# A fused attention and expert kernel: the written order of the first two batches replaced, v loaded behind k, no idle products

## The chip, the cores and the metric

The kernel runs on one core of one Trainium2 chip. A NeuronCore has five engines with instruction streams of their own: TensorE (PE, matrix products, with its weight loads shown as PEld), VectorE (DVE), ScalarE (ACT), GpSimd (POOL) and SyncE (SP, which here issues every DMA). The metric is the device time of one execution in microseconds, the median of several runs; smaller is better.

## The reference

Two attentions, then a layer with three gates, in float32:

```python
def sm_attn(qq, kk, vv):
    s = scale * np.matmul(qq, kk.transpose(0, 1, 3, 2))
    s = s - np.max(s, axis=-1, keepdims=True)
    a = np.exp(s)
    a = a / (np.sum(a, axis=-1, keepdims=True) + 1e-09)
    return np.matmul(a, vv)
p_packed = sm_attn(p, k, v)                 # 32 packed queries per head
out = sm_attn(q, p_packed, p_packed)        # 576 queries per head
x = out.transpose(0, 2, 1, 3).reshape(B * S, H * D)
h = np.maximum(np.maximum(x @ w1, x @ w2), x @ w3)
return h @ w_out
```

There are 8 batches of 8 heads, 576 positions and head dimension 64; w1 to w3 are 512 by 768 and w_out is 768 by 512.

## The kernel before, in words

All of the work of one batch is cut into stages. A stage is a Python generator that emits a few instructions at each step, and the order in which steps of different stages and batches are emitted is written out by hand as a text of words: START for all of batches 0 and 1 and the beginning of batch 2, and LOOP, which is run for each of the batches 2 to 7 with numbers relative to it. `run` (L619) reads the words. A word is a letter for the stage, digits for its batch (added to the loop's base) and its part, and perhaps a last letter for the engine of a step that has a choice: v for VectorE, g for GpSimd, a for ScalarE. Without that letter the step takes a default. Each engine runs its instructions in the order in which they were emitted, so this text sets every queue. The words stand for:

- k, v, q, w: loads on SP's queue. One k tile (L159) holds keys and packed queries of half the heads (640 KB), one q tile (L174) 576 KB, one v pair (L165, L166) 512 and 64 KB, one w tile (L153) 512 KB of raw weights, three for each of the six parts of w1 to w3 and six more for w_out. w tiles have six buffers in turn; k, v, q and several intermediate results share eight.
- C: a raw w tile is turned into float32 without a table: two ScalarE steps (L188, L193), a shift on VectorE (L202), an integer add on GpSimd (L206).
- S: scores of the packed queries (L253, tiles s1, two halves r = 0 and 1). A: maximum (L266, L267) and exponential (L271), then, for batches 0 and 1, transposes on TensorE (L296, L297) and copies (L129 on ACT, L131 on DVE). X: from batch 2 on the transposes go by VectorE (L313) and sixteen small DMAs (L319). Z: reciprocal (L282, L283). V: value products (L337) and their scaling (L347). K: transpose of the packed result (L352) and a copy to pt.
- Q: products of q with the packed result (L366). B: the second softmax, in blocks of 32 (L389 to L412), its result split into a rounded high and a low part (a2h, a2l).
- P: the packed result times part j of the weights (L439), split in ph and pl (L450, L452). N: the layer products mi (L475), three for each of the two halves r, because high times high, low times high and high times low are added up; 216 for a batch. E: the maximum over three gates (L489). H: sums and differences of quarters and their splits, O: the products with w_out (L544, mo) in the seven-product scheme of Strassen, F: their sums and the stores. W prepares w_out for that.
- I and J with a count of 128-column blocks: idle products. `rouse` (L138) multiplies the identity with itself into a PSUM tile that the next real product overwrites. I arms it ahead of the next stage's products, J emits it at once. START has I10, J9, J6, three times J2, J11 and J21.

PSUM has a pool of four tiles of one bank ("moe": mi, mo, and some pw) and one of two tiles of two banks ("big").

Of the kernel before, what the change touches and what calls it, by code (L numbers as in the profile page):

```python
# [45 lines left out]


START = """
k00 k01 I10 S0 A00 A00 J9 A00 q00 A00 w00 A01 A01 v00 J6 A01 v01 Z01 C00 C00 Z00 w02 C02 A01v V00 C00 V00 q01
V01 V01 J2 K0 C00 w01 w10 K0 C02 C02 J2 Q0 B010 C02 B010 B010v C01 C01 w11 B010 C10 C01 C01 Q0 w12 C10 B001  # L50
B000 B001 B000 B001v B000v C10 C10 C11 C11 C11 B000 C11 B000 B010 w20 C12 J11 P00 P00 w22 B011 P00 B000 B000
C12 B011 B001 P00 C12 C12 J21 P01 k10 B000 B000 B010 B001 C20 w32 k11 w21 B000 B000 B010 B001 N00 B010 B010
B010g C22 C22 P01 P00 B010 N00 B001 B011v B001g v11 J2 S1 v10 B011 P01 C32 C32 N01 N01 N01 C20 B011 w30 E000v
C22 B011v B001 E010 A11 A11 A10 A10 E010 Z11 B001v C21 C20 C21 C22 N00 B001v B011 E000 A10 A11 q10 A10v E000
q11 A11 N00 B011g B011 B011 V101 C20 C30 C30 w31 B011 Z10 E010 N01 V101 C21 C21 K1 C30 N00 w52 C31 K1v C32 C32
Q1 N00 E011 E001 B10 C31 w41 P02 P02 B11 C52 P10 P10 B10 w40 B11 k20 C40 C41 C31 P02 N01 E011 C30 N01 C31 P03
B10 P03 E001 E001 C41 N02 N02 E020 N02 C52 N02 E011 k21 N02 H00 w42 B10 B11 P10 E021 P03 S2 C40 E020 C40 N03
N03 N03 v21 C41 C41 C42 E020 B11 C42 B10 E021 C52 E030 C42 A20 A20 A21 A21 w50 C50 w51 B11 B11 B10 X2 X2 C50
C50 C51 N02 C52 N03 C40 C42 P04 C51 C50 B10 E030 E030 P11 B11 N03 B11g N03 C51 B10g P04 C51 P04 E031 N04 N04
N04 P05 E031 B11 v20 B11 E040v E040 B10 H01 H01v N04 N04 N04 E021 w61 C61 E031 P05 E041 P05 N05 N05 N05 E040  # L60
w60 C60 B10g B10 B11 H00 N10 C61 E041 P11 Z20 E050 H00v X2 C60 C60 E041 C61 E050 P11 V201 Z21 V201 N11 N11 K2
w64 N10 C61 E110v E110 E050 H01 H01 w65 C65 C65 N11 q21 N11 N10 K2 E100v N10 H04v H04 q20 Q2 N11 w62 N10 E111
E110 C60 W0v N10 W0v W0v W0 w63 W0 H02v H02 E101 C65 P13 H04v B20 E100 B21 E101 C65 W0 E111 E100 P12 N11 C62
C62 C63 C63 P13 C62 P12 W0v H03 C64 N05 C63 E101 N05 N05 C63 E051v P12 E051 C64 C64 P13 N12 N12 E111 C62 H01
H03v W1v W1v W1v N13 H02v N13 N13 E120 E130 P14 W1 P15 P15 E130 N12 C64 W2 W2 E051 N12 E121 W1v N13 E131 E130
P14 W2v W2g W0 P15 E120 E120 N13 E131 W2v N12 E121 N12 E121 W0g W0 H05g P14 W2g O0 O0 W1 W2v B21 W2 N14 N14
W1v B20 N13 E131 H03 H05 F0 E140 O0 E140 F0 N14 E140 H12v H03v O0 k31 F0 N14 H05 N14 N15 N15 N15 B20v H11 H05v
E141 N14 E141 H01v W2 H10v W1v E150 B21v E150 E141 H03 F0 H03v W1g N15 N15 E151 E151 O0 H10g H10v H05 O0 H05v
O0 B21 E150 W2 F0 F0 H13 H13 N15 E151 H14v O0 F0 F0 O0 B20 F0 O0 O0 B20 W1v H12 O0 F0 H12 H14 H11 F0 F0 F0 O0
H13v O0 H13v H13 H14 P20 P20 P22 F0 F0 H15 P21 H11v B21 F0 H15v P22 O1 O1 F1 k30 P20 O1 O1 O1 O1 P21 H15v H15v  # L70
H11v H15 H13v P22 H11g H11v B20v H15v O1 P20 F1 O1 B20 B20g O1 O1 O1 F1 O1 F1 B21 B21 F1 F1 B21g F1 O1 F1 P20
B20 B20v O1 F1 F1 F1 B21 F1 F1 P21 F1 F1 B21 B21 B20v F1
"""


LOOP = """
S1 A10 N00 E000 A11 N01 v10 E010v A10 N00 N00 N00 N00 N00 X1 A11 X1 v11 N02 N02 N02 N02 N02 E000 X1 Z10 E001
E001 E001 N01 E020 E020 E020 E000 H00 N01 N01 E010 E010 N01 E021 E021 H00g N01 H00 N02 P05 E011v E011 E011
H01v H01 P03 k21 P04 V101 E021 P03 P03 P03 P03 H01 P04 N03 P04 N03 q11 H02 H01 Z11 V101 P04 P04 N04 E040 P05
K1 N03 N03 N03 N03 H01v N04 N04 H01 q10 E030v E030 E030 H02g E031 K1 Q1 E031 N04 E041 H02 P05 N05 E031 E040  # L80
E040 N04 N04 B11 N05 N05 E050 B10 B10 B10v N05 N05 H03g H03 E051 E041 E041 N05 B11 P10 H03 H04v H04 H03 H03
E050 E050 B10 E051 E051 H05 P10 H04v B11 P11 H03v B11 P12 P12 O0 O0 F0 O0 F0 B10 H05v H05 B11 H05v B11 B11 B11
H05g B10 P11 O0 H05 O0 B10 k20 B10g P10 O0 F0 P10 P10 F0 B11 B11g P11 O0 O0 F0 F0 F0 O0 B10 O0 B11 O0 F0 F0 F0
B10g O0 O0 P12 O0 F0 F0 F0 F0 F0 B10v F0
"""


# [604 lines left out]
```

## Time and profile before

| | us |
|---|---|
| time, median of 3 runs | 466.14 (465.88 to 466.8) |
| span of the profiled execution, first to last instruction | 464.4 |
| PE busy in that span | 455.2 |
| VectorE busy | 333.5 |
| GpSimd busy | 247.9 |
| ScalarE busy | 159.9 |
| PE products at L143 (idle products) | 12.9 in tiles of their own, 3.8 ahead of the first scores |

The profiled execution is given by its span; the time of the runs holds what lies around the span too. A row of a timeline gives start, duration, engine, line, operation, output and inputs, and in brackets the idle time before it and what ended it. A row of the chain gives start, duration, engine, tile and line. In a row of a stretch of the span the figures are the length, then the busy time (and instructions) of PE, PEld, DVE, ACT and POOL, the granted clock, the DMA share and GB/s. The trace holds two instructions for each float32 product.

### The profile page before, as it was taken

What the parts mean: (1) busy time and instruction counts of PE and PEld (TensorE: products, weight loads), DVE (VectorE), ACT (ScalarE), POOL (GpSimd) and SP (SyncE); (2) the same over time, 40 slices, a digit from 0 to 9 for tenths busy, and PEclk for the clock granted to TensorE, in tenths of its full rate; (3) what the DMA queues carried; (4) which work ended last, traced back from release to release, by engine and by line L of the source; (5) the groups of instructions that cost most, each with busy time, mean ns of one, the idle gap of its engine ahead of it and who ended that gap; (6) DMA issues with size and microseconds to landing.
All of it is one profiled execution on the core that took longest, in us unless ns stands there. A gap on an engine that the chain in (4) does not pass through costs nothing.

```text
span 464.4 us, 11561 instructions
## 1 busy us (share of the span) xinstructions
PE 455.2 (98%) x4724; PEld 404.9 (87%) x4724; DVE 333.5 (72%) x698; ACT 159.9 (34%) x341; POOL 247.9 (53%) x213
## 2 busy tenths in 40 slices
PE   7999998999999999999999999999999999999996
PEld 3477887899899898998899988998989988998996
DVE  1799987888887678566887479766786668845552
ACT  2787856535322126022331025121260223302130
POOL 0468875574542675526572384706764275725832
PEclk9999999999999999999999999999999999999999
DMA  8999846010316430256004450065202540020002
GB/s 313 398 382 355 321 98 230 1 58 25 95 66 195 135 119 1 80 160 233 2 27 152 87 211 2 27 199 155 94 1 94 151 116 1 28 76 1 2 6 97
DMA packets 35780, 55.66 MB, mean 120 GB/s; under 512 B 17296, under 2 KB 26512, under 8 KB 35728
## 3 DMA queue, kind: packets, MB, share of 16 engines
q1 hardware_dynamic: 35728, 54.93, 35.4%
q8 instruction: 37, 0.61, 0.5%
q14 instruction: 15, 0.12, 0.1%
HBM read 41.94 MB, written 9.44 MB: 111 GB/s over the span
## 4 chain that ended last, share of the span: by engine, by line
PE 88%; DMA 5%; SPq 3%; DVE 3%; issue 1%; ACT 1%; DVEq 0%
PE mi L475 44%; PE mo L544 29%; PE pw L439 6%; PE idle L143 2%; SPq L319 2%; PE s L366 2%; PE av L337 2%; DMA wi<-in_wi 2%; PE s L253 2%; DMA q<-in_qt 1%; DMA kt<-in_kp 1%; PE tp L296 0%; DMA xt<-x 0%; SPq L159 0%; PE pa L337 0%
## 5 line engine op out<-in xcount | busy, mean ns | idle before, releaser
L475 PE MATMUL mi<-a2h,ph 128*128 128x288 f32 x576 | 173.5, 301 | 0.8 <-DVE pl L452 0.6
L475 PE MATMUL mi<-a2l,ph 128*128 128x288 f32 x576 | 169.9, 295 | 0.0
L475 PE MATMUL mi<-a2h,pl 128*128 128x288 f32 x576 | 169.6, 295 | 0.0
L489 DVE TENSOR_TENSOR r<-mi,r 128x288 f32<-128x288 f32 x192 | 84.4, 452 | 57.8 <-PE mi L475 55.3
L475 PEld LDWEIGHTS mi<-a2h,ph 128*128 128x128 f32 x576 | 108.0, 188 | 13.4 <-issue 7.0
L475 PEld LDWEIGHTS mi<-a2l,ph 128*128 128x128 f32 x576 | 108.0, 188 | 0.2
L475 PEld LDWEIGHTS mi<-a2h,pl 128*128 128x128 f32 x576 | 108.1, 188 | 0.0
L513 POOL TENSOR_TENSOR r<-r 128x288 f32<-128x288 f32 (+1 forms) x47 | 50.4, 1083 | 81.3 <-DVE r L489 65.5
L129 ACT COPY r<-mi 128x288 f32<-128x288 f32 x73 | 29.0, 399 | 185.8 <-PE mi L475 185.7
L450 ACT ACTIVATE ph<-pw 128x384 fp32r<-128x384 f32 (+1 forms) x67 | 40.2, 631 | 46.5 <-PE pw L439 43.5
L452 DVE SCALAR_TENSOR_TENSOR pl<-pw,ph 128x384 fp32r<-128x384 f32 (+1 forms) x67 | 46.2, 713 | 9.5 <-ACT ph L450 9.2
L544 PE MATMUL mo<-ych,xl 128*128 128x288 f32 x144 | 42.5, 295 | 0.0
L544 PE MATMUL mo<-ych,xh 128*128 128x288 f32 x144 | 42.4, 294 | 0.0
L544 PE MATMUL mo<-ycl,xh 128*128 128x288 f32 x144 | 42.3, 294 | 0.0
L439 PE MATMUL pw<-w_sb,pt 64*32 64x384 f32 x768 | 36.3, 487 | 0.1
L206 POOL TENSOR_TENSOR w_sb<-w_sb,wi 128x512 int32<-128x512 int32 x18 | 23.9, 1336 | 22.0 <-DVE w_sb L202 17.4
L134 POOL TENSOR_TENSOR ybl<-r,ybh 128x576 fp32r<-128x576 f32 x15 | 21.7, 1448 | 19.7 <-DVE ybh L131 16.2
L134 POOL TENSOR_TENSOR ycl<-r,ych 128x864 fp32r<-128x864 f32 x12 | 26.6, 2218 | 5.1 <-PE mi L475 2.4
L544 PE MATMUL mo<-yah,xh 128*128 128x288 f32 x96 | 28.9, 301 | 0.0
L544 PE MATMUL mo<-yal,xh 128*128 128x288 f32 x96 | 28.4, 296 | 0.2 <-DVE yal L134 0.2
L544 PE MATMUL mo<-ybh,xh 128*128 128x288 f32 x96 | 28.3, 295 | 0.0
L544 PE MATMUL mo<-yah,xl 128*128 128x288 f32 x96 | 28.3, 295 | 0.0
(123 smaller groups left out, 808.4 us busy)
## 6 DMA issues: line engine op xcount, KB each, us to landing
kt<-in_kp SPq DMA_DIRECT2D x16, 640.0 KB, 5.4
q<-in_qt SPq DMA_DIRECT2D x16, 576.0 KB, 5.6
wi<-in_wi SPq DMA_DIRECT2D x18, 512.0 KB, 8.6
v<-in_va SPq DMA_DIRECT2D x16, 512.0 KB, 5.7
wi<-in_wo SPq DMA_DIRECT2D x6, 512.0 KB, 6.7
out_t<-r SPq DMA_DIRECT2D x8, 288.0 KB, 2.2
out_t<-t SPq DMA_DIRECT2D x8, 288.0 KB, 2.3
out_t<-s SPq DMA_DIRECT2D x8, 288.0 KB, 2.7
```

The costliest lines, as they stand in the source:

```text
L129: e.copy(out=out, in_=src)
L134: on(default).tensor_tensor(out=lo, in0=src, in1=hi.bitcast(F32), op=ALU.subtract)
L143: nc.tensor.matmul(out=ps[:, 0:n * P], lhsT=ident, rhs=ident.unsqueeze(1).to_broadcast([P, n, P]), start=True, stop=True,)
L206: nc.gpsimd.tensor_tensor(out=dst.bitcast(I32), in0=dst.bitcast(I32), in1=up, op=ALU.add)
L253: nc.tensor.matmul(out=s1[b][r][32 * n:32 * n + 32, hf, 0:HS], lhsT=kt[g][o, w:w + NP], rhs=kt[g][o, pr * S + hf * HS:pr * S + (hf + 1) * HS],
L439: nc.tensor.matmul(out=ps[r][NP * n:NP * n + NP, 0:NW * P], lhsT=pt_sb[b % 2][o, NP * n:NP * n + NP], rhs=w_sb[o, j, n * NW * P:(n + 1) * ...
L450: nc.scalar.activation(out=hi[:, r], in_=x, func=AF.Copy, scale=2.0 ** -WS)
L452: nc.vector.scalar_tensor_tensor(out=lo[:, r], in0=x, scalar=2.0 ** -WS, in1=hi[:, r].bitcast(F32), op0=ALU.mult, op1=ALU.subtract,)
L475: nc.tensor.matmul(out=sums[b, j, hf, x][:, 0:HS], lhsT=w[:, r, x * P:(x + 1) * P], rhs=a[:, c], start=(r == 0 and n == 0), stop=(r == R - ...
L489: nc.vector.tensor_tensor(out=h, in0=sums[b, j, hf, i][:, 0:HS], in1=h, op=ALU.max)
L513: less = lambda out, x, y: on("g").tensor_tensor(out=out, in0=x, in1=y, op=ALU.subtract)
L544: nc.tensor.matmul(out=ps[:, 0:HS], lhsT=w[:, x, m * P:(m + 1) * P], rhs=h[:, z], start=(p == 0 and i == 0), stop=(p == NQ - 1 and i == 2),)
```

## The change

START is written anew. The stages, their number of steps and the functions are the same; the order of the words, and for many steps the engine letter, are not. The words I10, J9, J6, J2 (three times), J11 and J21 are left out, so no idle product is emitted. In LOOP the order is the same and some words get an engine letter which is the default of that step. Nothing else differs, apart from one more line in START, so every line number behind it is one higher.

```diff
 START = """
-k00 k01 I10 S0 A00 A00 J9 A00 q00 A00 w00 A01 A01 v00 J6 A01 v01 Z01 C00 C00 Z00 w02 C02 A01v V00 C00 V00 q01
+k00 k01 S0 A01 w02 C02 C02 w01 C02 A00 A00 v00 v01 A01 C01 C01 C01 A01 Z00 A01v C01 w00 A00 A00a q00 V01 C00
...
 LOOP = """
-S1 A10 N00 E000 A11 N01 v10 E010v A10 N00 N00 N00 N00 N00 X1 A11 X1 v11 N02 N02 N02 N02 N02 E000 X1 Z10 E001
+S1 A10 N00 E000a A11 N01 v10 E010v A10 N00 N00 N00 N00 N00 X1 A11 X1 v11 N02 N02 N02 N02 N02 E000 X1 Z10 E001a
```

SP's queue, the first loads before (kt are k tiles; wi0_2 is part 0, third tile 2; the tile's number in the program ends a name):

```order
L159 DMA kt0_79<-in_kp 128x1280
L159 DMA kt1_81<-in_kp 128x1280
L174 DMA q0_122<-in_qt 128x1152
L153 DMA wi0_0_127<-in_wi 128x512
L165 DMA v0_136<-in_va 128x1024
L166 DMA v0_136<-in_vb 64x256
L165 DMA v1_149<-in_va 128x1024
L166 DMA v1_149<-in_vb 64x256
L153 DMA wi0_2_160<-in_wi 128x512
L174 DMA q1_189<-in_qt 128x1152
L153 DMA wi0_1_216<-in_wi 128x512
L153 DMA wi1_0_218<-in_wi 128x512
```

and now:

```order
L160 DMA kt0_79<-in_kp 128x1280
L160 DMA kt1_81<-in_kp 128x1280
L154 DMA wi0_2_105<-in_wi 128x512
L154 DMA wi0_1_109<-in_wi 128x512
L166 DMA v0_119<-in_va 128x1024
L167 DMA v0_119<-in_vb 64x256
L166 DMA v1_122<-in_va 128x1024
L167 DMA v1_122<-in_vb 64x256
L154 DMA wi0_0_145<-in_wi 128x512
L175 DMA q0_157<-in_qt 128x1152
L175 DMA q1_186<-in_qt 128x1152
L154 DMA wi1_1_240<-in_wi 128x512
```

Both q tiles of batch 0 move back to the end of the first eleven issues; the v tiles keep their places, with two w tiles and no q tile between them and k.

PE's queue in the opening, before, from the last score product to the first value products (idle6 and idle14 are idle products, tp and pa the transposes of a1):

```order
L253 MATMUL s1_0_1_84<-kt1_81 32x288
L143 MATMUL idle6_111<-ident_67 128x512 x2
L143 MATMUL idle6_111<-ident_67 128x128
L296 MATMUL tp0_0_115<-ident_67,a1_0_0_108 128x128 x4
L297 MATMUL pa0_0_116<-ident_67,a1_0_0_108 64x128
L143 MATMUL idle14_139<-ident_67 128x512
L143 MATMUL idle14_139<-ident_67 128x256
L296 MATMUL tp0_1_142<-ident_67,a1_0_1_133 128x128 x4
L297 MATMUL pa0_1_143<-ident_67,a1_0_1_133 64x128
L337 MATMUL pa0_0_116<-v0_136,a1t0_0_124 32x64 x2
```

and now:

```order
L254 MATMUL s1_0_1_84<-kt1_81 32x288
L297 MATMUL tp0_1_131<-ident_67,a1_0_1_125 128x128 x4
L298 MATMUL pa0_1_132<-ident_67,a1_0_1_125 64x128
L297 MATMUL tp0_0_147<-ident_67,a1_0_0_116 128x128 x4
L298 MATMUL pa0_0_148<-ident_67,a1_0_0_116 64x128
L338 MATMUL pa0_1_132<-v0_119,a1t0_1_141 32x64 x2
```

The idle products are gone, and the half r = 1 is transposed and multiplied with v ahead of r = 0.

VectorE's queue at its beginning, before:

```order
L266 TENSOR_REDUCE mx0_0_104<-s1_0_0_83 128x1
L267 TENSOR_SCALAR nm0_0_105<-mx0_0_104 128x1
L266 TENSOR_REDUCE mx0_1_129<-s1_0_1_84 128x1
L267 TENSOR_SCALAR nm0_1_130<-mx0_1_129 128x1
L282 TENSOR_SCALAR z1_0_1_134<-z1_0_1_134 128x1
```

and now:

```order
L267 TENSOR_REDUCE mx0_1_101<-s1_0_1_84 128x1
L268 TENSOR_SCALAR nm0_1_102<-mx0_1_101 128x1
L203 TENSOR_SCALAR w_sb_72<-wi0_2_105 128x512
L267 TENSOR_REDUCE mx0_0_112<-s1_0_0_83 128x1
L268 TENSOR_SCALAR nm0_0_113<-mx0_0_112 128x1
```

The maximum of r = 1 is taken first, and a shift of a w tile stands between the two maxima.

More of the change, by code (lines that the diff above doesn't have):

```diff
@@ L48 @@
 START = """
-k00 k01 I10 S0 A00 A00 J9 A00 q00 A00 w00 A01 A01 v00 J6 A01 v01 Z01 C00 C00 Z00 w02 C02 A01v V00 C00 V00 q01
[L50 to L72, printed above, removed]
+k00 k01 S0 A01 w02 C02 C02 w01 C02 A00 A00 v00 v01 A01 C01 C01 C01 A01 Z00 A01v C01 w00 A00 A00a q00 V01 C00
@@ new lines @@
+Z01 C00 C00 C00 q01 V01 V00 V00 K0 K0v Q0 Q0 B000 B000 B010 B010 C02 w11 C11 C11 C11 B010v B001 B000g B000
+B011 C11 B000 w10 C10 C10 C10 C10 P00 P00 P00 B011 w30 B000a B000 P00 B010 B010 B010v w12 C12 C12 C12 C12 P01
+B000v B000 P00 w22 B010 C22 C22 B001 B000a B000v B010v B010 B010v B010g k10 P01 P01 N00 C22 C30 C30 N00 B011v
+C30 B011 B001v C30 w21 k11 S1 A10 E000a A11 B011 C22 B011v B011 B011g N01 N00 w20 C20 N01 E010v A10 A10 B001
+E000 A11 C21 B001 B001v B001 A10a E010 A11 A11a v11 B001v B001 B011 B001v N01 v10 V101 B001v N00 B011a B011g
@@ new lines @@
+Z10 Z11 V101 K1 E010 q10 C21 C21 C21 N00 K1a q11 Q1 C20 C20 C20 w32 C32 B10 B11 w31 C32 C31 C31 C31 C31 C32
+C32 B11 w42 E000 E001a N00 E001 E001 P10 P02 N01 N01 N01 w40 P03 C42 P02 P02 B11g N02 N02 E011a E011 E011 w41
+k21 C40 P10 P10 C41 C41 C41 C41 N02 P03 P03 C42 k20 S2 C42 C42 E020a w52 C52 C40 C40 E020 N03 C52 A20 A20 N03
+N03 P11 C52 A21 A21 E030v E030 C40 P04 N02 w60 C60 N02 X2 X2 Z21 E030 N02 C52 N03 w51 N03 N03 E020 C51 C51 C51
+H00g w50 C50 C50 C50 C50 E021a w65 P04 B10 E021 B11 E021 H02v C60 P04 N04 B11 B11v N04 v21 E031a B10g C51 B10
@@ new lines @@
+B10 B10v N04 C60 B11 B11v E040a E040 E040 P05 Z20 C65 v20 E031 E031 H01a H01g N04 E041v N04 w62 C62 N04 C60
+P05 P05 N05 N05 C62 P11 X2 V201 B10 B10v B10 E050a N05 w61 B11 B11a B10a w63 E041 E041 N05 N05 C61 C61 B11v
+H00g B10v N10 C61 V201 K2 H00g H01g E050 P11 C61 N05 E051a E100a W0v E051 E051 W0g W0v N11 E110a N11 K2a q21
+q20 W0a W0g Q2 W0v W0v N11 N11 w64 W0g B21 P13 B21 C64 B20 P12 N11 N11 E111v C62 C62 E050 H05g P12 H03a E111
+N10 E111 H01g C65 E110 N10 N10 N10 N10 E110 C65 C65 E100 P12 N12 P13 P13 N13 E101a E101 E101 P14 C63 C63 B21g
@@ new lines @@
+H03v E100 P15 N12 N12 C64 C64 C63 W0v P14 P14 H04g H04a B20 E120a E120 E120 H02a C63 B21 B21 E130v N14 N14 N14
+N14 W1g E140v E140 E140 E141a H02g N14 N14 W1v W1g E141 N12 N12 N12 H04v E141 P15 C64 E121a W2g P15 H05g N13
+N13 N13 N13 W1a E121 E121 W2g W2v W2a E131a N15 W1v W1v W1v W1g E150a E130 E130 N15 N15 W2v H05g W2a E150 W0g
+N15 N15 N15 E151a E151 E151 H05g H01a W2v N13 E131 E131 k31 H03v H05a H05v H03v H03v H03v O0 F0 O0 O0 F0 H01v
+W2g O0 O0 O0 F0 F0 F0 H12v E150 H13a H13g F0 O0 F0 O0 O0 H10g W2a F0 W1v F0 H12a H10a H12g H13v H13v O0 O0 O0
@@ L73 @@
+k30 H14v W1v F0 W2g O0 O0 P20 P21 B20v F0 F0 B20 H14a B20 F0 F0 H13a F0 F0 P22 H14v H10v O1 O1 H11v H11v H11v
+H15a H15v H15v H15v O1 P21 P20 P20 H13v H11v H11v B21a H11v F1 H15a O1 O1 F1 O1 B21 B21g H15v O1 B20a B20 P22
+O1 O1 F1 F1 F1 O1 B20g P21 F1 F1 B20 F1 F1 B20g B20v F1 F1 F1 P22 O1 F1 O1 B21 B21g B21g P20 P20 O1 O1 F1 F1
+F1
 """
 LOOP = """
-S1 A10 N00 E000 A11 N01 v10 E010v A10 N00 N00 N00 N00 N00 X1 A11 X1 v11 N02 N02 N02 N02 N02 E000 X1 Z10 E001
-E001 E001 N01 E020 E020 E020 E000 H00 N01 N01 E010 E010 N01 E021 E021 H00g N01 H00 N02 P05 E011v E011 E011
@@ L79 @@
[L79 to L83, printed above, removed]
@@ L84 @@
-B10g O0 O0 P12 O0 F0 F0 F0 F0 F0 B10v F0
+S1 A10 N00 E000a A11 N01 v10 E010v A10 N00 N00 N00 N00 N00 X1 A11 X1 v11 N02 N02 N02 N02 N02 E000 X1 Z10 E001a
+E001 E001 N01 E020a E020 E020 E000 H00g N01 N01 E010 E010 N01 E021a E021 H00g N01 H00g N02 P05 E011v E011 E011
+H01v H01g P03 k21 P04 V101 E021 P03 P03 P03 P03 H01g P04 N03 P04 N03 q11 H02g H01g Z11 V101 P04 P04 N04 E040a
+P05 K1 N03 N03 N03 N03 H01v N04 N04 H01g q10 E030v E030 E030 H02g E031a K1a Q1 E031 N04 E041a H02g P05 N05
+E031 E040 E040 N04 N04 B11 N05 N05 E050a B10 B10 B10v N05 N05 H03g H03g E051a E041 E041 N05 B11 P10 H03g H04v
@@ L85 @@
+H04a H03g H03a E050 E050 B10 E051 E051 H05a P10 H04v B11g P11 H03v B11 P12 P12 O0 O0 F0 O0 F0 B10 H05v H05g
+B11 H05v B11a B11 B11v H05g B10a P11 O0 H05g O0 B10 k20 B10g P10 O0 F0 P10 P10 F0 B11 B11g P11 O0 O0 F0 F0 F0
+O0 B10 O0 B11g O0 F0 F0 F0 B10g O0 O0 P12 O0 F0 F0 F0 F0 F0 B10v F0
 """
```

## The prediction

> **What bounds the kernel now.** I read the page first, then the chain of work that ended last, then the timelines of single engines in the opening. The page names the engine:
>
> ```profile
> PE 455.2 (98%) x4724; PEld 404.9 (87%) x4724; DVE 333.5 (72%) x698; ACT 159.9 (34%) x341; POOL 247.9 (53%) x213
> PE   7999998999999999999999999999999999999996
> PEclk9999999999999999999999999999999999999999
> DMA  8999846010316430256004450065202540020002
> ```
>
> TensorE (PE) is busy from end to end, so only PE time spent on nothing useful can be won or lost: waits, and the idle products of L143. The chain shows where that time is:
>
> ```profile
> 7.16 1.17 PE s L253 x24
> 8.33 2.13 PE idle L143 x6
> 12.53 0.66 PE tp L296 x4
> 13.29 1.77 PE pa L337 x80
> 16.26 1.16 PE s L366 x32
> 17.42 2.56 PE idle L143 x6
> 19.98 1.19 PE pw L439 x16
> 21.16 4.71 PE idle L143 x12
> 25.87 1.07 PE pw L439 x16
> 26.94 1.92 PE mi L475 x12
> 28.86 0.43 PE idle L143 x2
> 29.29 1.13 PE s L253 x32
> ...
> 65.49 1.93 DMA xt<-x
> 67.47 1.51 PE av L337 x74
> ...
> 69.49 6.43 DMA q<-in_qt
> ...
> 76.06 1.21 PE s L366 x32
> ...
> 142.87 14.51 PE mi L475 x108
> ```
>
> Up to 26.94 us PE mostly fills time with idle products while batch 0 goes through scores, softmax, values, queries and the second softmax. From the first layer products (mi) on it is dense, with one visible hole, in which the query products of batch 2 wait for their data:
>
> ```profile
> 76.06 1.21 PE L366 MATMUL s<-q,pt 64*32 64x288 f32 x32 [1.28 <-DMA q<-in_qt]
> ```
>
> So PE arrived there at 74.78 (76.06 less 1.28).
>
> **What can change at all.** The letters added in LOOP only write out the default engine of a step, so the loop's instructions stay as they are. In START the same stages run the same number of times, and from the second half of batch 0's Strassen product 6 on the useful PE work stands in the same order, but for two projections that trade places. The change is therefore the time that PE loses before that point. I measure it at batch 2's query products, called Q2. In the new order 12 mi products fewer stand ahead of Q2 (all other PE work ahead of it is equal), and they follow behind it. At 14.51/108 = 0.134 us each they are 1.6 us. So change = (new start of Q2) + 1.6 - 76.06, if what follows runs as densely as before. That execution spans 464.4 us and the median of the runs is 466.14, 1.7 above, which I leave as it is and add the change to the median. A change under 0.2% (0.93 us) can't be told from none.
>
> **The clock of the array.** The idle products do one thing. The very first ones against later ones, all 128 rows by up to 512 columns, and the weight loads of their passes:
>
> ```profile
> 1.36 3.83 PE L143 MATMUL s<-ident 128*128 128x512 f32 x6 [1.36 <-POOL ident masks.py:199]
> 3.23 0.34 PEld L143 LDWEIGHTS s<-ident 128*128 128x128 f32 x1 [0.52 <-issue]
> 4.08 0.28 PEld L143 LDWEIGHTS s<-ident 128*128 128x128 f32 x1 [0.52 <-issue]
> 8.26 2.21 PE L143 MATMUL idle<-ident 128*128 128x512 f32 x6
> 9.23 0.19 PEld L143 LDWEIGHTS idle<-ident 128*128 128x128 f32 x1 [0.24 <-issue]
> 9.66 0.19 PEld L143 LDWEIGHTS idle<-ident 128*128 128x128 f32 x1 [0.24 <-issue]
> ```
>
> At 3 to 4 us one pass follows another after 0.85 us (3.23 to 4.08), at 9 us after 0.43 (9.23 to 9.66), and a weight load takes 0.34 against 0.19. An array that has just begun works at half pace, and got to full pace after some 3 us without a pause. The PEclk row shows 9 all the same, so it does not tell this state. [...]
>
> **The opening, step by step.** Two sums, one with PE at full pace, one at half.
>
> Scores. Their last 24 instructions begin at 7.16 when the second k tile lands; the two k loads stay first, so this stays. Full pace: end 8.33. Half: twice 1.17, end 9.5.
>
> First softmax and transposes. The rows:
>
> ```profile
> 8.39 0.76 DVE L266 TENSOR_REDUCE mx<-s 128x1 f32<-128x576 f32 x1 [8.39 <-PE s L253]
> 10.03 0.15 DVE L267 TENSOR_SCALAR nm<-mx 128x1 f32<-128x1 f32 x1
> 11.64 0.74 ACT L271 ACTIVATE a<-s,nm 128x576 f32<-128x576 f32 x1
> 14.03 0.41 DVE L202 TENSOR_SCALAR w_sb<-wi 128x512 uint32<-128x512 uint32 x1
> ```
>
> Two maxima with their scalings take 1.79 (8.39 to 10.18). The new order puts one weight shift of 0.41 between them and runs both exponentials (0.74 each) behind them, with no copy between, and the transposes after both: 8.33 + 1.79 + 0.41 + 1.48 + 0.1 = 12.1 at full pace (12.53 before), 13.3 at half.
>
> Values to queries. From 12.53 to 16.26 it took 3.73, with the first half of the value products beside a copy. Now both halves stand behind the copy: half of 1.77 is 0.9 more, 4.6 in all. Full pace: 16.7. Half pace adds 0.6 for the first transposes (0.66 doubled) and between 0 and 1.8 for the value products (80 short ones, perhaps bound by issue and not by the array; I take 0.9, the middle): 19.4.
>
> The q data. Loads run one behind another, so a landing can be read from the bytes ahead. ACT rows of w conversions that waited for data, and the POOL add that ends one:
>
> ```profile
> 14.79 0.68 ACT L188 ACTIVATE wi<-wi 128x512 f32<-128x512 f32 x1 [1.18 <-DMA wi<-in_wi]
> 17.49 0.68 ACT L188 ACTIVATE wi<-wi 128x512 f32<-128x512 f32 x1 [0.78 <-DMA wi<-in_wi]
> 18.95 1.29 POOL L206 TENSOR_TENSOR w_sb<-w_sb,wi 128x512 int32<-128x512 int32 x1 [0.86 <-DVE w_sb L202]
> ```
>
> The tile of the first row ends the queue's first 4032 KB, that of the second its first 5120 (k 640, q 576, w 512, v 576 KB each): 1088 KB in 2.7 us, 403 KB/us. In the new order the second q tile stands at the end of exactly 5120 KB, since v and two more w tiles are ahead of it, so it lands at 17.45. At full pace that, not the 16.7, starts the queries: 17.45, 1.2 later than before. At half pace it is hidden: 19.4.
>
> To the first mi. PE's queue holds the second projection ahead of it, which needs w1_2. That load ends 7168 KB, 2048 behind, so 17.45 + 5.1 = 22.5. From landing to the end of its POOL add took 17.45 to 20.24, 2.8, for the row above: 25.3, and half a projection (1.07/2): 25.8 at full pace. Before: 26.94. At half pace the softmax steps, which share ACT and DVE with this conversion, are 1.95 later (19.4 less 17.45), so mi begins at 27.75.
>
> To the end of batch 1's scores. Twelve mi took 1.92, the scores 1.13. Full pace: 27.7, then the last k tile, at the end of 9472 KB in both orders (six w and two k tiles behind the 5120), at 17.45 + 4352/403 = 28.25; end 29.4. At half pace: does mi still run so? Between the projections PE now has nothing for several us (7.3 us of idle products stood there). No row shows an array that pauses. The bounds are 0 and 12 x 0.134 = 1.6, and 0 and 1.1 for the scores. The nearest row is the array's first start, at half pace, so I take the full 1.6, and 0.5 for the scores, by when it may be released: 27.75 + 1.92 + 1.6 + 1.13 + 0.5 = 32.9. Before: 29.29 + 1.13 = 30.42. [...]
>
> To Q2. Before, 74.78 - 30.42 = 44.4; less 1.6 of mi is 42.8. Half pace: 32.9 + 42.8 = 75.7, so change +1.3. Full pace: 29.4 + 42.8 = 72.2, if the data are there. The x spread of 16 small issues is released by batch 2's maxima, which come a microsecond earlier too, but now one w load more is issued ahead of it, and q stands behind it (65.49, 69.49); I allow 0.7 of wait, 72.9, change -1.6.
>
> Everything else (engine letters on other steps, w loads renumbered between 20 and 60 us) I cost at nothing: PE has its dense work over it. If that cover is gone, a late w tile costs up to its conversion, 2.8.
>
> **The rivals.** First, the forecast: half pace at the opening and again at the first mi, 466.14 + 1.3 = 467.4; for it speak the doubled passes and the idle products gone (2.13, 2.56, 4.71 and 0.43 us in the chain); own range 466.3 to 469. Chance 0.47.
>
> The array is not slowed (bursts of scores, transposes and values are enough): then batch 0's chain ends earlier and batch 2's q wait shrinks, 464.5, own range 463.3 to 465.4. This is the faster side. It decides if mi begins before 26.5. For it: full pace came after only 3 us of work. Against: no stretch that long now stands ahead of 13 us. Chance 0.30.
>
> Half pace only at the opening, full by mi (the 4 us of transposes and values release it and it lasts): 1.6 and 0.5 fall away, +1.3 - 2.1 = -0.8, 465.3 to 466.2 with data waits, no change. Chance 0.13.
>
> VectorE becomes the bound behind Q2. All mi of batch 1 now stand ahead of the first mo product, which before were mixed, and mi feeds DVE most. The row of that stretch:
>
> ```profile
> 80.00:100.00 20.00, 19.73 (x188) 17.37 (x173) 18.61 (x33) 9.79 (x18) 12.43 (x14) 1.00 0.00 1
> ```
>
> DVE is third: 18.61 of 20 us. Ten per cent more would overfill it by 0.5 us in 20; over the 30 us of batch 1's 216 products that is 1 to 3, so with the cold opening about 470. Against it: the 108 mi in a row of the loop run without a wait (14.51). Chance 0.10. That the idle products stay is no rival: none is left in the new order.
>
> **How the numbers follow.** Faster: the second case and a little of the third, 0.32. Same: the third and the near edge of the forecast, 0.19. Slower: 0.49. Time 467.4, the likeliest case. As both signs hold much of the chance, the range runs from 463.6, inside the full-pace case, to 469.4, above the forecast's own, leaving out most of the DVE case.
>
> **What would show it.** Scores ending near 9.5 and not 8.3; query products at 19.4 or at 17.45; first mi at 27.8 or 25.8, and the first dozen 0.27 or 0.13 apart; Q2 at 75.7 or 73, with or without a wait for q; DVE at 100% between 80 and 105. I am wrong if mi begins before 26.5 at full pace, or if new waits stand behind Q2.

## The result, and the profile after

The changed kernel takes 473.08 us (median, 472.57 to 474.32) against 466.41 (465.88 to 466.8): ratio 1.0148, 95% interval 1.0131 to 1.0166, 6.7 us slower. Forecast were 467.4 and a range up to 469.4. The sign is as forecast, the size is not, and the opening, which was given as the reason, carries a quarter of the loss: 1.75 of the 7.1 us by which the profiled execution is longer.

The page of the changed kernel, with the rows that stood for the kernel before in the prediction:

```profile
PE 448.3 (95%) x4684; PEld 401.0 (85%) x4684; DVE 336.9 (71%) x704; ACT 159.2 (34%) x337; POOL 244.6 (52%) x211
PE   2589998999999999999999999999999999999996
PEclk9979999999999999999999999999999999999999
```

PE now has holes in the first three slices (2, 5, 8 tenths where 7, 9, 9 stood), and the third slice shows a clock of 7 tenths. The opening on PE's timeline (start, duration, line, output and inputs, idle time before and what ended it):

```profile
6.49 2.14 PE L254 MATMUL s<-kt 64*32 64x288 f32 x24 [0.38 <-DMA kt<-in_kp]
12.69 1.09 PE L297 MATMUL tp<-ident,a 128*128 128x128 f32 x4 [4.05 <-ACT a L272]
...
18.56 1.21 PE L367 MATMUL s<-q,pt 64*32 64x288 f32 x32 [0.38 <-DVE pt L132]
...
24.84 1.51 PE L440 MATMUL pw<-w_sb,pt 64*32 64x384 f32 x8 [4.44 <-POOL w_sb L207]
...
28.17 0.61 PE L476 MATMUL mi<-a2h,ph 128*128 128x288 f32 x1
...
29.06 0.44 PE L476 MATMUL mi<-a2h,ph 128*128 128x288 f32 x1
29.30 0.44 PE L476 MATMUL mi<-a2h,pl 128*128 128x288 f32 x1
...
30.48 0.30 PE L476 MATMUL mi<-a2h,ph 128*128 128x288 f32 x1
...
30.97 1.20 PE L254 MATMUL s<-kt 64*32 64x288 f32 x32
```

Scores at half pace (2.14 for what took 1.17), transposes too (1.09 for 0.66), queries at full pace (1.21 for 1.23). Then PE stands 4.44 us, and the first mi come 0.24 us apart (29.06 to 29.30) until 30.26, from 30.48 on 0.14. Here the granted clock in stretches of 4 us shows it as well (the last three figures of a row are clock, DMA share, GB/s; from 20 to 24 the clock was 0.95):

```profile
24.00:28.00 4.00, 2.77 (x16) 0.40 (x16) 3.90 (x13) 2.53 (x5) 2.18 (x2) 0.50 1.02 410
28.00:32.00 4.00, 4.00 (x48) 3.12 (x44) 2.83 (x7) 3.12 (x6) 1.52 (x2) 0.70 1.06 347
```

So the opening went nearly as forecast. Most of the loss comes later. The table follows the starts of PE's stages on its timeline (the chain of work puts the same stages up to 0.07 us later); S are scores, Q query products, the number is the batch, S3 the first stage of LOOP. In the new order 6 mi fewer stand ahead of Q1 and 12 fewer ahead of S2 and Q2, at 0.134 us each; what they would take is added.

| stage | before | after | later | mi left for later | lost so far | lost in this stretch |
|---|---|---|---|---|---|---|
| S1 | 29.22 | 30.97 | 1.75 | 0 | 1.75 | 1.75 |
| Q1 | 38.90 | 40.96 | 2.06 | 0.8 | 2.86 | 1.1 |
| S2 | 49.53 | 50.72 | 1.19 | 1.6 | 2.79 | -0.1 |
| Q2 | 76.06 | 79.22 | 3.16 | 1.6 | 4.76 | 2.0 |
| S3 | 141.67 | 147.52 | 5.85 | 0 | 5.85 | 1.1 |
| end | 464.4 | 471.5 | 7.1 | 0 | 7.1 | 1.25 |

The chain of work that ended last runs, before Q2, no longer over the spread and q but over VectorE's queue (start, duration, engine, tile, line):

```profile
55.78 1.34 DVE x L314 x2
...
69.00 1.84 DVE e L410
...
75.78 1.02 PE mi L476 x6
...
79.29 1.24 PE s L367 x32
```

Between S2 and Q2 VectorE (third pair of figures, behind PE and PEld) is busy for 26.68 of 28.48 us. The changed kernel:

```profile
50.72:79.20 28.48, 25.95 (x306) 21.84 (x305) 26.68 (x57) 17.41 (x35) 16.85 (x14) 1.00 0.72 227
```

and the kernel before:

```profile
49.50:76.06 26.56, 25.15 (x307) 21.85 (x307) 23.14 (x52) 16.80 (x34) 18.25 (x15) 1.00 0.70 229
```

It looks as if VectorE, which the new letters give more work (the multiplication L410 of batch 1's second softmax among it), had become the bound ahead of Q2. The experiments show a second chain, the way to q, that ends there at nearly the same time.

### The profile page after: what moved, and what is told of

It is laid out like the page before. It is cut to its first block, busy times and chain, and to the rows that moved or that the text cites. A ratio compares the mean times of both kernels' runs of the same rounds, so it can differ in the third digit from the quotient of the medians.

```text
span 471.5 us, 11485 instructions
## 1 busy us (share of the span) xinstructions
PE 448.3 (95%) x4684; PEld 401.0 (85%) x4684; DVE 336.9 (71%) x704; ACT 159.2 (34%) x337; POOL 244.6 (52%) x211
## 4 chain that ended last, share of the span: by engine, by line
PE 83%; DVE 9%; SPq 2%; DMA 2%; issue 1%; ACT 1%; POOL 0%; DVEq 0%; ACTq 0%
PE mi L476 41%; PE mo L545 29%; PE pw L440 6%; PE s L254 2%; SPq L320 2%; PE s L367 2%; DVE r L490 2%; PE av L338 1%; DVE mx L267 1%; DMA kt<-in_kp 1%; DVE pl L453 1%; DVE x L314 1%; PE pa L338 1%; DVE et L413 0%; DVE e L410 0%
## 5 line engine op out<-in xcount | busy, mean ns | idle before, releaser
L514 POOL TENSOR_TENSOR r<-r 128x288 f32<-128x288 f32 (+1 forms) x49 | 52.8, 1087 | 81.3 <-DVE r L490 65.1
L440 PE MATMUL pw<-w_sb,pt 64*32 64x384 f32 x768 | 37.9, 495 | 5.7 <-POOL w_sb L207 4.8
L135 POOL TENSOR_TENSOR ybl<-r,ybh 128x576 fp32r<-128x576 f32 x15 | 21.7, 1444 | 23.7 <-DVE ybh L132 16.1
L440 PEld LDWEIGHTS pw<-w_sb,pt 64*32 64x32 f32 x768 | 12.8, 106 | 20.5 <-issue 9.2
```

The source lines that it names most:

```text
L135: on(default).tensor_tensor(out=lo, in0=src, in1=hi.bitcast(F32), op=ALU.subtract)
L440: nc.tensor.matmul(out=ps[r][NP * n:NP * n + NP, 0:NW * P], lhsT=pt_sb[b % 2][o, NP * n:NP * n + NP], rhs=w_sb[o, j, n * NW * P:(n + 1) * ...
L514: less = lambda out, x, y: on("g").tensor_tensor(out=out, in0=x, in1=y, op=ALU.subtract)
```

## The experiments

Eighteen kernels ran. Each is compared with the kernel before, 466.3 to 466.6 beside them. The first expectations weigh theory A (the array's clock: the missing idle products) against theory B (VectorE, by the letters of batch 1's second softmax). Later ones give each theory that they weigh a letter and say what it is.

### The idle products: given back, and taken out of the old order

Given back to the changed kernel:

```diff
-k00 k01 S0 A01 w02 ...
+k00 k01 I10 S0 A01 w02 ...   J14 ahead of the third A01, J1 ahead of K0 and Q0, J18 ahead of the first P01
```

> The changed kernel with idle products put back at five places (I10 ahead of the first scores, J14 between scores and transposes, J1 on either side of the packed transpose, J18 ahead of the second projection), nothing else. The changed kernel took 473.1 us, the kernel before 466.4. Theory A (the array's half pace at the opening and at the first layer products): those rows return to full pace (scores 1.2 us instead of 2.2, layer products 0.13 us apart from the first on), batch 1's scores end 1.7 to 2.5 us earlier than at 32.1 us, and the time falls by as much, to 470.6 to 471.4; if the clock were all of the loss, to 466.5. Theory B (VectorE holds TensorE up between batch 2's scores and its query products, because the new order gives it steps that GpSimd did): the opening gets shorter, but the wait on VectorE takes most of it back, 472 to 473.

Taken out of the kernel before (I10, J9, J6, J2, J2, J11, J21, J2), nothing else changed:

> The kernel before without its idle words (I10, J9, J6, J2, J2, J11, J21, J2), in its own order. Theory A: the array runs at half pace in the opening and in the first layer products, which costs 2 to 3.5 us: 468.4 to 469.9. Theory B (the loss lies in the order and its engine letters, not in the clock): 466.4 to 467.3.

Measured: 472.16 (ratio 1.0122, 1.0108 to 1.0136) and 469.67 (1.0063, 1.0050 to 1.0077). The first lies where theory B put it, the second where theory A did. The missing idle products alone cost the old order 3.3 us, but given back to the new order they are worth only 0.9, and the intervals of the two kernels just overlap. The new order with its idle products is still 5.7 us behind: the two losses overlap. The trace of the first run shows where the gain goes. Batch 1's scores start at 28.83, 2.1 us earlier than in the changed kernel, and then PE meets data that isn't as much earlier:

```profile
49.01 1.21 PE L254 MATMUL s<-kt 64*32 64x288 f32 x32 [0.36 <-DMA kt<-in_kp]
...
77.50 1.21 PE L367 MATMUL s<-q,pt 64*32 64x288 f32 x32 [0.58 <-DMA q<-in_qt]
```

Q2 is 1.7 us earlier, S3 only 0.7, after one more wait of 1.05 for pl at 132.

### Which idle products

The kernel before without the first five (up to the queries of batch 0), and without the last three (ahead of the layer products):

```diff
-k00 k01 I10 S0 A00 A00 J9 ... v00 J6 ... V01 V01 J2 K0 ... C02 J2 Q0
+k00 k01 S0 A00 A00 ... v00 ... V01 V01 K0 ... C02 Q0
```

```diff
-C12 J11 P00 ... C12 J21 P01 ... v11 J2 S1
+C12 P00 ... C12 P01 ... v11 S1
```

> The kernel before without the first five idle products (I10, J9, J6, J2, J2, up to the query products of batch 0), those ahead of the layer products kept (J11, J21, J2). Theory H (the half pace costs only where PE sets the end: the opening is hidden behind the w tiles' conversion, and what costs is the cold start of the layer products): first mi at 27.0 to 27.6 instead of 26.9, time 466.5 to 467.4. Rival (the opening is the dear part, as its chain is the critical one): 468.3 to 469.7, all of what leaving out all of them cost.

> The kernel before with the first five idle products, without the three ahead of the layer products (J11, J21 and the last J2). Theory H: PE stands still for several us between the projections and runs the first layer products at half pace: batch 1's scores 1.2 to 2 us later than in the kernel before, time 467.5 to 468.6. Rival (the opening is the dear part): 466.3 to 467.0.

Measured: 468.63 (1.0043, 1.0026 to 1.0061) and 467.92 (1.0030, 1.0014 to 1.0045). The second is as theory H had it; the first isn't, it lies in its rival's range, and the opening costs 2.0 us by the ratio. Part of that is the experiment's own: the idle products that stay are counted for an earlier start, and now hold PE up themselves. On PE's timeline of that run:

```profile
19.47 2.63 PE L143 MATMUL idle<-ident 128*128 128x512 f32 x6
...
23.24 4.78 PE L143 MATMUL idle<-ident 128*128 128x512 f32 x12
27.95 0.98 PE L439 MATMUL pw<-w_sb,pt 64*32 64x384 f32 x16
```

No wait stands between the queries at 18.33 and the first mi at 28.87, 2.0 later than before: the queries came 2.1 late, and the fixed fill stands behind them. So this run doesn't tell how dear a cold opening is by itself. In the run without the last three the granted clock falls, from 1.00 (16 to 20 us) to 0.50 (24 to 28), though PE pauses only 2.30, 1.66, 0.22 and 0.90 us at a time. Its mean of 0.69 from 20 to 24 puts a single fall at 21.5 us, half a microsecond into the second pause. The two longest, and the stretch behind them:

```profile
20.10 0.87 PE L439 MATMUL pw<-w_sb,pt 64*32 64x384 f32 x12 [2.30 <-POOL w_sb L206]
22.62 1.49 PE L439 MATMUL pw<-w_sb,pt 64*32 64x384 f32 x4 [1.66 <-POOL w_sb L206]
```

```profile
24.00:28.00 4.00, 2.88 (x14) 0.39 (x12) 3.90 (x13) 3.07 (x9) 2.98 (x4) 0.50 1.02 411
```

In the changed kernel the clock fell at 23.6 us (1.00 until 23.6, 0.50 from 23.7 on), 3.2 us into the pause of 4.44. In this run no pause is longer than 2.30: that pause, a projection of 0.87 us and half a microsecond of the next pause stood ahead of the fall. So the length of one pause alone doesn't tell when the clock falls.

### v behind k, alone

```diff
-k00 k01 I10 S0 A00 A00 J9 A00 q00 A00 w00 A01 A01 v00 J6 A01 v01 Z01
+k00 k01 v00 v01 I10 S0 A00 A00 J9 A00 q00 A00 w00 A01 A01 J6 A01 Z01
```

> The kernel before with its idle products, and only the first loads changed: batch 0's v directly behind its k, so that the first q tile and the first w tile land 1152 KB later. One of the three parts of the change by itself. Theory M (the first w conversions start only behind the softmax of batch 0, and the first layer products wait for a w tile that stays where it is in the queue): 466.1 to 467.0, no change. Rival: the first w tile's conversion and with it the first projection come later by what 1152 KB take, up to 2.7 us, part of it hidden: 467.2 to 468.5.

466.53 (1.0002, 0.9991 to 1.0013): nothing. The edit goes further than the change, in whose queue two w tiles still stand between k and v and it is the q tiles that move back. So it shows that the old order doesn't need its first q and w tile any earlier, and no run moves the q tiles of batch 0 as the change does.

### Old opening, new rest, and the other way round

Both kernels' words were cut behind batch 1's scores (S1) and joined crosswise. The first has the old words, idle products too, up to S1 and then what is left of the new ones; the second the new words up to S1 and then what is left of the old.

```diff
-k00 k01 S0 A01 w02 ... w21 k11 S1 A10 E000a A11 ...
+k00 k01 I10 S0 A00 A00 J9 ... B001g v11 J2 S1 w30 P01 C22 ... A10 E000a A11 ...
```

```diff
-k00 k01 I10 S0 A00 A00 J9 ... B001g v11 J2 S1 v10 B011 ...
+k00 k01 S0 A01 w02 ... w21 k11 S1 w20 B001 B001 ... B001g v11 v10 C32 ...
```

> A mixed order: the words of the kernel before, idle products included, up to and with batch 1's scores; from there on the words of the new order that are left, in their order. Theory A: batch 1's scores end near 30.4 us as before, and what is left of the loss is small, 466.5 to 468.5. Theory B: the opening's 1.7 us are won, but from batch 2's scores on VectorE sets the pace as in the changed kernel and the loss there and behind stays, 469.5 to 471.5.

> The changed kernel's words up to and including batch 1's scores, then the kernel before's words for what is left, no idle product. The complement of the run with the old opening. Theory D (two separate losses: a cold opening of 1.75 us up to batch 1's scores, and some 4 us behind them from the new order and letters): batch 1's scores at 31.0 as in the changed kernel, batch 2's query products some 1.7 to 2.5 us later than before, time 468 to 469. Rival (the cold opening also delays the loads and the conversions, and that is what costs the time behind the scores): the loss behind the scores stays, 472 to 473.

475.12 (1.0190, 1.0176 to 1.0204) and 472.11 (1.0112, 1.0091 to 1.0133). The first is above both theories' ranges, and the second lies with theory D's rival. But a join makes waits of its own: in the first, PE stands 2.83 us until 35.42 for a copy on ScalarE, which is queued behind a weight conversion that waits for its load.

```profile
24.07 9.38 DMA wi<-in_wi
...
33.53 0.67 ACT wi L189
...
35.09 0.29 ACT r L130
...
35.42 1.29 PE mi L476 x6
```

In the second, S1 comes at 32.06 and Q1 11.0 us behind it (9.7 in the kernel before), and 2.1 us more are lost behind S3. So the totals say little, but the stretches do. From S2 to Q2 the first takes 28.6 us and the second 26.4; the changed kernel takes 28.5, the kernel before 26.5. From Q2 to S3 the second takes 65.7, as the kernel before (65.6). The 3 us that the changed kernel loses in these two stretches belong to the new words in them, not to a late start.

### Letters and order

The changed kernel with the letters of three steps of batch 1's second softmax turned back: the addition on ScalarE, the multiplication and the low part on GpSimd, as before.

```diff
-B11v ... B10v ... B11v ... B10v B10 ... B11v ... B10v
+B11a ... B10a ... B11g ... B10g B10 ... B11g ... B10g
```

> The changed kernel with six engine letters of batch 1's second softmax set as they were before (the scaling by the reciprocal and the low part on GpSimd, the addition of 1e-9 on ScalarE, for both halves), still without idle products. Theory B: VectorE loses about 3.2 us of work between 63 and 74 us (1.8 for two scalings and 1.2 for two low parts), the wait of 1.1 us ahead of the mi product at 75.8 us goes, and the time falls by 1.5 to 3 us, to 470.1 to 471.6. Theory A: nothing of that stretch sets the end, 472.6 to 473.6.

480.29 (1.0294, 1.0278 to 1.0309): 7.2 us slower than the changed kernel, the opposite of theory B. VectorE has 3.1 us less to do between S2 and Q2, and yet PE waits longer for it. PE and VectorE:

```profile
82.90 0.40 PE L476 MATMUL mi<-a2h,ph 128*128 128x288 f32 x1 [2.62 <-DVE r L490]
```

```profile
82.05 0.42 DVE L219 TENSOR_TENSOR xt<-xb 128x256 f32<-128x256 f32 x1 [3.80 <-POOL xb L207]
82.39 1.01 DVE L490 TENSOR_TENSOR r<-mi,r 128x288 f32<-128x288 f32 x2
```

The maximum r, for which mi waits, is ready to run, but in VectorE's queue it stands behind a step of the w_out preparation, and that waits 3.80 us for GpSimd, whose queue now holds the softmax steps ahead of it. The letters fit this order; those of these three steps can't be turned back by themselves. All letters turned back, and the new ones put into the old order (112 words each; the first of them):

```diff
-A00 A00a q00 ... K0 K0v Q0 ... B000g ... B000a
+A00 A00 q00 ... K0 K0 Q0 ... B000v ... B000
```

```diff
-q00 A00 w00 ... K0 C00 w01 w10 K0 ... B000v ... B000
+q00 A00a w00 ... K0 C00 w01 w10 K0v ... B000g ... B000a
```

> The changed kernel's order of words, each step with the engine that the kernel before gives it (112 words of START change their letter), no idle product. Theory D (behind batch 1's scores VectorE is the bound, because the new letters put 3.5 us more on it between batch 2's scores and its query products and 3.5 more up to the loop): VectorE's busy time up to the loop falls back by 4 us, the waits for pl, r and the exponential at 56 to 76 us go, time 468.5 to 470.5. Rival O (the order itself costs: all layer products of batch 1 ahead of the first mo, and GpSimd's queue is written for the new letters): no better than the changed kernel, 472 to 480.

> The kernel before's order of words and its idle products, each step with the engine that the changed kernel gives it. Letters alone. Theory D: VectorE has 3 to 4 us more up to the loop and PE waits for it, time 468.5 to 470.5. Rival O (letters cost nothing without the order they were made for, or cost only by head-of-line waits in queues): 466 to 467, or well above 471 if queues block.

491.73 (1.0538, 1.0518 to 1.0558) and 481.03 (1.0314, 1.0287 to 1.0341). Theory D's 468.5 to 470.5 is missed by both; rival O had the direction of both, and not the size of the first. So with the order fixed, the other kernel's letters cost 14.5 us (old order) and 18.7 us (new order). In the old order with the new letters PE waits 1.28 for r, 1.45 for pl and later 1.68 for r, where the kernel before waits 0.25 for r once up to the loop.

### Less work on VectorE

The multiplication of batch 1's second softmax left out, in the changed kernel and with the idle products given back:

```diff
-        on("v").tensor_tensor(out=e3, in0=e3, in1=z.unsqueeze(2).to_broadcast([P, nt, NP]), op=ALU.mult)
+        if b != 1:
+            on("v").tensor_tensor(out=e3, in0=e3, in1=z.unsqueeze(2).to_broadcast([P, nt, NP]), op=ALU.mult)
```

> The changed kernel without the multiplication of batch 1's second softmax by its reciprocals (L410, two VectorE instructions, 2.6 us between 64 and 71 us in the changed kernel); the result for batch 1 is therefore not normalised. Takes work off VectorE and puts it nowhere. Theory D (VectorE is the bound between 52 and 76 us): the wait of 1.09 for r at 75.8 goes, batch 2's query products 1.5 to 2.5 earlier than in the changed kernel, time 470.5 to 471.7. Rival (the stretch is bound by data, GpSimd or ScalarE, VectorE only follows): 472.6 to 473.5.

> The changed kernel with its idle products given back and without the multiplication of batch 1's second softmax (L410, two VectorE instructions; the result of batch 1 isn't normalised). Theory C: only VectorE's chain gets shorter; the wait for r goes and the wait for q grows by as much: query products still 28.5 behind batch 2's scores, time 471.8 to 472.4. Theory D: 0.5 to 2 us earlier, 470 to 471.6.

473.81 (1.0141, 1.0116 to 1.0167) and 471.78 (1.0108, 1.0089 to 1.0126); the changed kernel and its run with idle products had 473.08 and 472.16. The second time lies between the two theories' ranges, so the stretch decides: S2 to Q2 takes 28.5 us in both runs, as without the edit. Theory D falls: 2.6 us less on VectorE bring nothing, since PE now waits for q instead. PE in the first of the two:

```profile
75.77 0.37 PE L477 MATMUL mi<-a2h,ph 128*128 128x288 f32 x1 [0.55 <-DVE r L491]
79.79 1.21 PE L367 MATMUL s<-q,pt 64*32 64x288 f32 x32 [0.51 <-DMA q<-in_qt]
```

VectorE's queue and the way to q end within about half a microsecond of each other, and with VectorE relieved q holds Q2 at 28.5. The converse, q relieved and VectorE not, was not reached: the run that tried it (below) made other things late.

### The way to q

SP's queue in that stretch, before (x16 is the spread of x):

```profile
44.97 0.46 SPq L165 DMA_DIRECT2D v<-in_va  x1
...
49.92 2.67 SPq L153 DMA_DIRECT2D wi<-in_wo  x2
54.84 11.26 SPq L319 DMA_DIRECT2D xt<-x  x16
...
68.93 0.88 SPq L174 DMA_DIRECT2D q<-in_qt  x2
```

and in the changed kernel:

```profile
52.84 0.42 SPq L166 DMA_DIRECT2D v<-in_va  x1
...
53.89 0.53 SPq L166 DMA_DIRECT2D v<-in_va  x1
...
55.03 0.75 SPq L154 DMA_DIRECT2D wi<-in_wo  x1
57.19 12.12 SPq L320 DMA_DIRECT2D xt<-x  x16
...
72.13 0.88 SPq L175 DMA_DIRECT2D q<-in_qt  x2
```

The new order loads batch 2's v behind several w tiles, which wait on SP for free buffers, and so v and one more w tile, 1664 KB, stand directly ahead of the 16 small transfers. Counted from S2: first issue at 5.3 before and 6.5 after (+1.2), spread 11.3 and 12.1 (+0.9), spread's end to q's issue 2.8 and 2.8, q's issue to Q2 7.1 and 7.1. That sums to the 2.0 lost. Within its spread SP now waits for the w load that stands last ahead of it (us in total, times, longest):

```profile
SPq L320 <- DMA wi<-in_wo: 1.3, 1, 1.3
```

In the changed kernel with its idle products, and in the one without the multiplication, the chain that ended last runs over this load, which lands 8.5 and 8.1 us behind its issue. Of the transfers in this stretch, the first eight of the spread, 40 KB each, before and after (median us from issue to landing last):

```profile
xt<-x SPq DMA_DIRECT2D x8, 40.0 KB, 2.2
```

```profile
xt<-x SPq DMA_DIRECT2D x8, 40.0 KB, 4.6
```

A part of that load order, the two v tiles (1152 KB) without the w tile, put into the kernel before (v21 and v20 directly ahead of the third X2):

```diff
-N03 v21 C41 ... B11 v20 B11 E040v ... E050 H00v X2 C60
+N03 C41 ... B11 B11 E040v ... E050 H00v v21 v20 X2 C60
```

> The kernel before with its idle products, and one thing of the changed kernel's load order: the two v tiles of batch 2 (1152 KB) stand directly ahead of the spread of x instead of four and two loads earlier. Theory Q (the 2.0 us that the changed kernel lost between batch 2's scores and its query products belong to the chain scores, x, spread on SP, value products, q load: 1.2 until the first of the 16 issues, 0.9 within them, as they wait for a load that stands right ahead of them): the spread takes 12 to 13 us instead of 11.3 or starts up to 1 us later, q's wait at the query products grows from 1.3 to 2.0 to 3.5, time 467.2 to 468.8. Theory D (VectorE bounds that stretch in the changed kernel, the load order is not the cause): 466.3 to 466.8.

468.20 (1.0040, 1.0025 to 1.0054): 1.9 us slower, and time and spread (12.69 us) are as theory Q had them. The wait for q didn't grow as it said; it fell to 0.84, and the value products wait for the spread instead. S2 to Q2 takes 27.6 us instead of 26.5, so 1.1 of the 1.9 show in this stretch of the profiled execution; 0.4 more came ahead of S1, where the words are the same. What SP waited for within the spread, and PE's rows:

```profile
SPq L319 <- DMA v<-in_va: 1.2, 1, 1.2
```

```profile
69.42 1.44 PE L337 MATMUL av<-v,xt 128*32 128x64 f32 x74 [0.53 <-DMA xt<-x]
...
77.57 1.25 PE L366 MATMUL s<-q,pt 64*32 64x288 f32 x32 [0.84 <-DMA q<-in_qt]
```

Which half decides in the new order, the first issue or the landing of the loads ahead? In the changed kernel with its idle products, C52, E030v and E030 were moved behind the two X2 that transpose x:

```diff
-P11 C52 A21 A21 E030v E030 C40 P04 N02 w60 C60 N02 X2 X2 Z21
+P11 A21 A21 C40 P04 N02 w60 C60 N02 X2 X2 C52 E030v E030 Z21
```

> The changed kernel with its idle products given back (472.16), and three words (a weight shift, 0.43 to 1.1 us on VectorE, a copy and a maximum of layer products, 0.45 each) behind the two transposes of batch 2's x instead of ahead of them. Tells the two halves of theory Q apart. If the first issue of the spread sets q: it comes 0.5 to 0.9 earlier, query products 27.6 to 28.0 behind batch 2's scores instead of 28.5, time 471.3 to 471.8. If the landing of the loads ahead of the spread sets it: the wait within the spread grows by what the first issue gains, 28.4 to 28.6, time 471.9 to 472.5.

472.48 (1.0127, 1.0107 to 1.0147). The spread starts 0.8 us sooner behind S2 (5.0 for 5.8) and takes 0.9 longer; Q2 is 28.5 behind S2 again, this time with PE waiting for VectorE and not for q:

```profile
53.51 13.59 SPq L320 DMA_DIRECT2D xt<-x  x16
```

So it is the loads ahead of the spread that set the spread's end in this order.

### Attempts at something faster

v20 and v21 ahead of w51, and the spread ahead of w62, in the changed kernel with its idle products; then the same without the multiplication:

```diff
-C52 N03 w51 ... N04 v21 E031a ... C65 v20 E031 ... N04 w62 C62 ... C62 P11 X2 V201
+C52 N03 v21 v20 w51 ... N04 E031a ... C65 E031 ... N04 X2 w62 C62 ... C62 P11 V201
```

> The changed kernel with its idle products given back (as in the run after_idle, 472.16), and two moves on SP's queue: the two v tiles of batch 2 ahead of the w load that stood two w loads before them (w51), and the spread of x of batch 2 (16 small issues) ahead of one w load (w62) that stood before it. Theory C (between batch 2's scores and its query products two chains end within 0.5 us of each other: VectorE's queue, and SP's chain of v and w loads, spread, q load): only SP's chain gets shorter, by 1.3 us or more; the wait of 0.58 for q at the query products goes, those of VectorE (0.59 for pl, 0.48 for r) stay: query products 27.9 behind batch 2's scores instead of 28.5, time 471.3 to 471.9. Theory D (VectorE alone bounds the stretch): 472.2, no change.

> Both edits at once: v tiles and spread earlier on SP's queue, and no multiplication of batch 1's second softmax (batch 1 isn't normalised). Theory C: both chains are shorter, and the gain is more than the sum of the two runs with one edit each: query products 27.0 to 27.5 behind batch 2's scores, time 470.3 to 471.2. Theory D: as without the multiplication alone.

477.44 (1.0235, 1.0220 to 1.0250) and 477.11 (1.0234, 1.0216 to 1.0253): 5 us slower than the run that they start from, and far from theory C's numbers. The spread itself takes 11.48 us here, about as in the kernel before (11.26) and 1.2 less than in the run that this one starts from (12.70), so without the loads directly ahead of it it is short in this order too. But w62, which is now issued behind the spread, lands at 70.8. Its conversion stands in ScalarE's queue ahead of a split ph, and PE stands still for 4.83 us until 72.30. ScalarE and PE:

```profile
70.90 0.65 ACT L189 ACTIVATE wi<-wi 128x512 f32<-128x512 f32 x1 [6.99 <-DMA wi<-in_wo]
72.30 0.61 PE L476 MATMUL mi<-a2h,ph 128*128 128x288 f32 x1 [4.83 <-ACT ph L451]
```

q comes later too: its issue waits 10.2 us for the value products, which stand behind these mi in PE's queue. So the spread couldn't simply be put ahead of w62. Whether v alone could be moved no run shows. In the kernel before, w64 behind batch 2's q, and, apart from that, x's transposes ahead of three softmax words:

```diff
-K2 w64 N10 C61 ... q21 ... q20 Q2 N11
+K2 N10 C61 ... q21 ... q20 w64 Q2 N11
```

```diff
-w51 B11 B11 B10 X2 X2 C50
+w51 X2 X2 B11 B11 B10 C50
```

> The kernel before with one word moved: the load w64 (512 KB of w_out) stands behind the q tiles of batch 2 instead of ahead of them. In the kernel before, the query products of batch 2 wait 1.28 us for q. Theory C, for the old order: that wait is a load's, 512 KB earlier in the queue is worth all of it, and nothing else is late there: time 465.1 to 465.6. Rival: another wait takes its place at once (yah on ScalarE, 1.0, in the run of this order without idle products), or the loop absorbs it: 466.2 to 466.6.

> The kernel before with three words of batch 1's second softmax (B11 B11 B10) behind the two transposes of batch 2's x instead of ahead of them, so that a VectorE reduction of 0.74 us no longer stands between the maxima and x. Theory Q (in the kernel before too the query products of batch 2 are released by the chain scores, x, spread, value products, q load): x and with it the spread start up to 0.5 us earlier, query products 26.0 to 26.4 behind batch 2's scores instead of 26.5, time 465.8 to 466.3. Rival (spread or q wait for something else): 26.5 again, or the softmax steps become late and it costs: 466.4 to 467.5.

466.75 (1.0005, 0.9988 to 1.0022) and 466.67 (1.0001, 0.9987 to 1.0015): no change, and neither theory C nor theory Q had it so. In both, Q2 still waits for q, 1.65 and 1.74 us: 512 KB ahead of q were not what made it late. In both, the first q load waits on SP some 2 us for the value products. In the second the spread begins 0.4 us sooner behind S2 (4.95 for 5.31) but ends no sooner (16.65 for 16.57). And in both profiled executions Q2 came later behind S2 than in the kernel before, 27.2 and 27.4 us for 26.5, so a difference of 0.9 in this stretch of one execution doesn't yet show in the median. No version that beats the kernel before was found.

## Why the prediction was wrong

**The opening** was right in kind and near in size. Scores ended at 8.7 (forecast 9.5; k landed 0.7 sooner than before), transposes began at 12.69 (13.3), queries at 18.56 (19.4), the first mi at 28.17 (27.75). That the later q tiles are hidden at half pace was right: the queries waited 0.38 us, for pt and not for q. That mi starts at half pace (0.24 us apart) was a guess between bounds and is shown. The full 1.6 for a dozen was a little much: nine ran slow, which cost 0.9, and batch 1's scores ended at 32.1, not 32.9. Of the forecast 2.5 us up to there, 1.7 came. How close that is holds some luck: with the same words up to there, S1 began 0.6 to 1.2 us later in three other runs.

**From batch 1's scores to Q2** is the step that failed: "44.4; less 1.6 of mi is 42.8". It took 47.1 (32.1 to 79.22). The 4.3 us between are the 1.28 of the old wait for q, which the sum let go, 1.1 between S1 and Q1, and 2.0 between S2 and Q2, less 0.1. Under the sum lay two things. "Everything else (engine letters on other steps, w loads renumbered between 20 and 60 us) I cost at nothing: PE has its dense work over it" is wrong twice. With the order fixed, the other letters cost 14.5 us and more, and the moved loads lengthen the spread by putting 1664 KB directly ahead of it; 1152 KB there alone cost the old order 1.9 us. The prediction saw one w load more ahead of the spread and not the two v tiles, and allowed for it only in the sum at full pace.

And PE's dense work doesn't cover a chain that goes once around all engines: Q2 hangs on S2 over maxima, x, 16 issues, value products and q, 26.5 us long before, with a wait of 1.28 at its end. (In the kernel before the maxima stood behind the shift of a w tile too, which ended 0.3 us after S2's products, so a load held the chain's beginning about as long as S2 did.) The prediction quoted that wait and took it for slack that might shrink. A wait for q at the end of the stretch meant that what was added to this chain, 2.0 us, was not hidden.

**Behind Q2** "if what follows runs as densely as before" was wrong by 1.1 us up to S3. The pauses there are small, 0.15 to 0.3 us each, at 82 and 104 to 109 us. No run isolates them; the stretch is 1.0 to 1.1 longer in the changed kernel and in the run with the old opening, and not in the run with the old words behind the new opening. The 1.1 between S1 and Q1 is open too: the chain runs there over VectorE's softmax steps of batch 0, and that they are the cause is argued and not shown.

**In the loop**, whose instructions are the same, 0.9 us were lost, and 0.35 behind it. Two passes took 54.66 and 54.20 instead of 54.03. In the first, one of the 16 issues of the spread took 1.80 us instead of 0.60:

```profile
262.59 1.80 SPq L320
```

Such an issue shows in some of the kernels (2.00 at 154 in the old order without idle products) and not in others. What causes it stays open.

**The rivals.** That VectorE becomes the bound was a rival with 0.10, but put behind Q2, for the mi in a row; there it was 8.4 and 9.0 of 10 us busy. It came to the limit ahead of Q2, where it was not looked for, and there as one of two chains that end together. Full pace at the opening (0.30) is refuted by the scores (2.14 us), full pace by mi (0.13) by the products 0.24 us apart.

**The size.** Leaving out the idle products alone costs 3.3 us, order and letters alone 5.7, both together 6.7. The first was forecast near its size (2.5 us up to batch 1's scores); the second was left out. About half of the loss in the profiled execution is traced to a cause, 1.75 us of the opening and 2.0 ahead of Q2; for the other 3.4 (1.1, 1.1 and 1.25) the place is known and the cause stays open.
